# Sorted attention and a mixture of experts in one program: earlier q heads, a shorter set-up path, and expert weights that wait for rows

## The chip, the cores and the metric

The kernel runs as one program on one core of one Trainium2 chip. The number that counts is the device time of that program in microseconds (us). The kernel before took 233.02 us as the median of three runs (231.26 to 235.55).

The engines are named as in the profile: PE is TensorE, with PEld for its weight loads; DVE is VectorE, ACT is ScalarE, POOL is GpSimd, SP is SyncE. A "q" behind a name (SPq, POOLq) is that engine's own instruction queue.

## The reference, cut to what matters

The program is two stages, one after the other. First comes an attention in blocks: a small matrix per head is normalised in rows and columns five times (Sinkhorn), blocks of k and v are mixed by it, and each of 8 blocks of 96 tokens attends to its own mixed block. Then a mixture of 8 experts works on the attention's output: each token goes to the one expert that its gate prefers.

```python
# q, k, v: (4, 8, 768, 64), sort_net: (4, 8, 8, 8); 8 blocks of 96 tokens
P = sort_net
for _ in range(5):
    P = P - max_row(P); P = exp(P)
    P = P / (row_sum(P) + 1e-09)
    P = P / (column_sum(P) + 1e-09)
k_sorted = einsum('bhij,bhjcd->bhicd', P, k_blocks)
v_sorted = einsum('bhij,bhjcd->bhicd', P, v_blocks)
attn = softmax(q_blocks @ k_sorted^T / sqrt(64))
x = (attn @ v_sorted) as (3072 tokens, 512)

# w_gate: (512, 8), modality_bias: (2, 8), w1: (8, 512, 1024), w2: (8, 1024, 512)
logits = x @ w_gate + modality_bias[modality_id]
e_idx  = argmax(logits)
gate_w = softmax(logits)[e_idx]
for e in range(8):
    h = relu(x[e_idx == e] @ w1[e])
    out[e_idx == e] = gate_w * (h @ w2[e])
```

## The kernel before

The attention is cut into 32 **units**: unit u works on two batches (g = u // 16), one half of the blocks, and one head (u % 8). Per unit, TensorE makes scores, ScalarE their exponential (L407), TensorE the product with v (`av`), and VectorE divides by the row sums, which writes 64 columns of the x tile `xb` (L424). Eight units fill one x tile of 8 x 96 tokens. The tile goes through the gate: four transposed pieces (`gate_T`) and four small products (`gate_L`), then `choose` and `place`, and its rows are scattered to a scratch array in HBM, sorted by expert, by eight indirect transfers of GpSimd. A `table` says which groups of 256 rows are full. Such a group is read back, transposed, as `xT`, and run through an expert. Experts are renumbered by the modality bias so that the two that will get nearly all tokens stand first; `home_pick` and `home_map` work this out. Slots 0, 2, 4, ... use the first one's weights, slots 1, 3, 5, ... the second one's.

The expert work is a list of **pieces**: `mL1` (8 matmuls of the first layer) and `mL2` (8 of the second). From unit 18 on, pieces are mixed in between the attention's steps.

```python
def load_q(g, hh):                      # four heads of two batches
    t = q_in(g, hh).rearrange("p (r h f) -> p r h f", r=2, h=4)
    return [nc.gpsimd.dma_start(out=t[:, par], in_=q[2 * g + par, 4 * hh:4 * hh + 4]
                                .rearrange("h (p t) d -> p h (t d)", t=6)) for par in range(2)][0]

def spread_q(g, hq, eng=None):          # reorders two heads in SBUF, L125
    ...
    for z in range(2):
        (eng or nc.vector).tensor_copy(il[:, z], t[:, :, (hq % 2) * 2 + z].rearrange("p r t d -> p t r d"))

load_q(0, 0)
...
load_k(0, 0); load_k(0, 1); load_v(0)
load_q(0, 1)
...
spread_q(0, 0, nc.gpsimd)
spread_q(0, 1, nc.gpsimd)
# ... cut ...
for u in range(4):
    tq_pe(u)                            # TensorE turns a head of q, L231
for it in range(5):                     # Sinkhorn on VectorE, exponential on ScalarE (L245)
    ...
    if it == 3: tq_out(0, nc.scalar.copy)
    if it == 4:
        for u in range(1, 4): tq_out(u, nc.scalar.copy)
    ...
make_bd(0)                              # block matrix of P for the sort, last line L276
# ... cut ...
def mod_rows():
    src = modI.rearrange("b (r t w) -> b t r w", r=16, t=6)[:, :, :, 0]
    nc.vector.tensor_copy(modB, src)                                    # L297
    tp = mipsum.tile([128, 64], BF16, tag="mi", name="modT")
    nc.tensor.transpose(tp[0:BLK, 0:NTL], modB..., ident[0:NTL, 0:NTL])  # L299
    nc.vector.tensor_copy(modF, tp[0:BLK, 0:NTL])

def gate_consts():
    red_w = perm_mult(wgf, wg_sb, "w")           # the gate's weights in the new order
    nc.gpsimd.tensor_scalar(modN, modF, -1.0, 1.0, ALU.mult, ALU.add)
    # ... three GpSimd operations make biasm, the bias of every token ...
    def rest_w():
        red_w()
        nc.vector.tensor_copy(wgp, wgf)
    return rest_w

def prep_s(u):
    if 4 <= u < 32 and not (u // 8) % 2 and u % 2 == 0:
        spread_q(u // 16, (u % 8) // 2)
        use(dve=0.7)
# ... cut ...
scores(0); expo(0)
home_pick(); home_map()
mod_rows()
load_k(1, 0); load_k(1, 1)
wait_w = gate_consts()
make_bd(1)
scores(1); expo(1)
late_consts()
...
for n, (f, g, x0, kd) in enumerate(g0[8:]):   # the sort of v, L358, copied out at L336
    f(g, x0, kd)
load_v(1); load_q(1, 0); load_q(1, 1)
zero_block()
av(0)
wait_w()
prep_s(4)
# ... cut: what is done at which unit ...
at2(9, place, 0)
for t in range(1, 8):
    at1(9 + t, lambda t: ones_[0](t), t)                 # scatter t of the first x tile
    if t == 3: at1(9 + t, lambda: load_w(0, parts=(0,)))
at1(16, table_x, 0)
at1(16, lambda: load_w(0, parts=(1,)))
at1(16, lambda: load_w(1))
at1(18, place, 1)
# ... cut ...
for u in range(2, 32):
    p1, p2 = pace(u)                    # (0, 0) below unit 18, then (1, u % 2)
    scores(u); expo(u)
    for f, a in A1.get(u, []): f(*a)
    run_pieces(p1)
    av(u - 1)
    prep_q(u + 2)
    prep_s(u + 3)
    for f, a in A2.get(u, []): f(*a)
    run_pieces(p2)
run_pieces(1); av(31)
run_pieces(2); gate_T(3, 3)
run_pieces(1); gate_L(3, 3); choose(3)
run_pieces(2); place(3)
for t in range(1, 8):
    run_pieces(2)
    ones_[3](t)
table_x(3)
run_pieces(1000)                        # all that is left
```

Of the kernel before, what the change touches and what calls it, by code (L numbers as in the profile page):

```python
# [17 lines left out]
def kernel(  # L18
# [13 lines left out]
    nc = tc.nc  # L32
# [80 lines left out]
    def load_v(g):  # L113
        nc.gpsimd.dma_start(out=v_in, in_=v_src[g * 128:(g + 1) * 128])

    def load_q(g, hh):
        t = q_in(g, hh).rearrange("p (r h f) -> p r h f", r=2, h=4)
        return [nc.gpsimd.dma_start(out=t[:, par], in_=q[2 * g + par, 4 * hh:4 * hh + 4]
                                    .rearrange("h (p t) d -> p h (t d)", t=6)) for par in range(2)][0]

    def spread_q(g, hq, eng=None):
        t = q_in(g, hq // 2).rearrange("p (r h t d) -> p r h t d", r=2, h=4, t=6)
        il = q_il[hq % 2].rearrange("p (h t r d) -> p h t r d", h=2, t=6, r=2)
        for z in range(2):
            (eng or nc.vector).tensor_copy(il[:, z], t[:, :, (hq % 2) * 2 + z].rearrange("p r t d -> p t r d"))  # L125
# [1 line left out]
    sI = singles.tile([128, 32], I32)  # L127
    pI = singles.tile([128, 1], I32)
    idI = singles.tile([BLK, NTL], I32)
    load_q(0, 0)  # L130
    nc.gpsimd.iota(sI, pattern=[[1, 32]], base=0, channel_multiplier=0)
    make_identity(nc, ident)
    load_k(0, 0)
    load_k(0, 1)
    load_v(0)
    load_q(0, 1)
    jI = singles.tile([1, 4], I32)
    hI = singles.tile([1, 4], I32)
    nc.gpsimd.iota(pI, pattern=[[0, 1]], base=0, channel_multiplier=1)
# [1 line left out]
    nc.gpsimd.iota(jI, pattern=[[1, 2], [0, 2]], base=0, channel_multiplier=0)  # L141
    nc.gpsimd.iota(hI, pattern=[[PR, 2], [CAP, 2]], base=0, channel_multiplier=0)
    spread_q(0, 0, nc.gpsimd)
    spread_q(0, 1, nc.gpsimd)

    ones_bf = singles.tile([128, 128], BF16)
    ones8 = singles.tile([128, E], FP32)
# [86 lines left out]
    def tq_out(u, eng):  # L234
        g, h = u // 16, u % 8
        qT = qTb[g][:, h * 768:(h + 1) * 768].rearrange("p (i t r) -> p i t r", i=NB, t=6)
        eng(qT, tq.pop(u).rearrange("p t (i r) -> p i t r", r=16))

    for u in range(4):
        tq_pe(u)  # L240
    for it in range(5):
        if it == 0:
            nc.vector.tensor_reduce(red, P_t, AX.X, ALU.max)
            nc.vector.tensor_tensor(P_t, P_t, red.broadcast_to([BH, NB, NB]), ALU.subtract)
        nc.scalar.activation(P_t, P_t, ACT.Exp)  # L245
        if it == 3:
            tq_out(0, nc.scalar.copy)
        if it == 4:
            for u in range(1, 4):
                tq_out(u, nc.scalar.copy)  # L250
        for f in gap[it]:
            f()
        nc.vector.tensor_reduce(red, P_t, AX.X, ALU.add)
        nc.vector.reciprocal(red, red)
        nc.vector.tensor_tensor(P_t, P_t, red.broadcast_to([BH, NB, NB]), ALU.mult)
        nc.vector.tensor_reduce(red, P_swap, AX.X, ALU.add)
        nc.vector.reciprocal(red, red)
# [41 lines left out]
        nc.tensor.transpose(tp[0:BLK, 0:NTL], modB.rearrange("b t r -> b (t r)"), ident[0:NTL, 0:NTL])  # L299
# [4 lines left out]
    def gate_consts():  # L304
        red_w = perm_mult(wgf, wg_sb, "w")
        nc.gpsimd.tensor_scalar(modN, modF, -1.0, 1.0, ALU.mult, ALU.add)
# [9 lines left out]
        def rest_w():  # L316
            red_w()
            nc.vector.tensor_copy(wgp, wgf)
        return rest_w

    busy = [0.0, 0.0]

# [54 lines left out]
        return u // 16, (u // 8) % 2, u % 8  # L377

    def prep_s(u):
        if 4 <= u < 32 and not (u // 8) % 2 and u % 2 == 0:  # L380
            spread_q(u // 16, (u % 8) // 2)
            use(dve=0.7)

    def prep_q(u):
        if 4 <= u < 32 and not (u // 8) % 2:
            tq_pe(u)
            tq_out(u, nc.scalar.copy if pick(0.8, 0.56) else nc.vector.tensor_copy)

# [220 lines left out]
    def w_views(z):  # L609
        o = z * WCOL  # L610
        return (w01[:, o:o + 4 * F].rearrange("p (c f) -> p c f", c=4),
                w01[:, o + 4 * F:o + WCOL].rearrange("p (c f) -> p c f", c=8))

    def load_w(z, tab=None, n=None, parts=(0, 1)):
        tb, n = (etab, z) if tab is None else (tab, n)
        er = nc.values_load(tb[0:1, n:n + 1], engines=(PoolEng,), min_val=0, max_val=E - 1)
        v1, v2 = w_views(z)
        if 0 in parts:
            nc.gpsimd.dma_start(out=v1, in_=moe_w1[bass.ds(er, 1)].rearrange("o (c p) f -> p (o c) f", p=128))
        if 1 in parts:  # L620
            nc.gpsimd.dma_start(out=v2, in_=moe_w2[bass.ds(er, 1)].rearrange("o (c p) f -> p (o c) f", p=128))

    def stage_of(s):
        return 0 if s < 2 else 1 if s < 4 else 2 if s < 8 else 3
# [1 line left out]
    xins = {}  # L626
# [99 lines left out]
    def late_consts():  # L726
        pt = singles.tile([128, 2], I32)
        nc.vector.tensor_scalar(pt[:, 0:1], pI, 15, None, ALU.bitwise_and)
        nc.vector.tensor_scalar(pt[:, 1:2], pI, 4, None, ALU.logical_shift_right)
        ptf = singles.tile([128, 1], FP32)  # L730
        ptc = singles.tile([128, 2], FP32)
        nc.vector.tensor_copy(ptc, pt)
        nc.vector.scalar_tensor_tensor(ptf, ptc[:, 0:1], 6.0, ptc[:, 1:2], ALU.mult, ALU.add)
        nc.vector.tensor_scalar(idI, idI, ptf[0:BLK], None, ALU.add)
        nc.vector.tensor_scalar(sF256, sF[0:1], float(PR), None, ALU.mult)
        nc.vector.tensor_copy(JC.rearrange("p a b -> p (a b)"), jI)
        nc.vector.tensor_copy(HC.rearrange("p a b -> p (a b)"), hI)
        use(dve=1.6)
# [9 lines left out]
    expo(0)  # L748
    home_pick()
    home_map()  # L750
    mod_rows()
    load_k(1, 0)
    load_k(1, 1)
    wait_w = gate_consts()
    make_bd(1)
    scores(1)
    expo(1)
    late_consts()
    use(dve=-busy[1], act=-busy[0])
    for n, (f, g, x0, kd) in enumerate(g0[8:]):  # L760
        f(g, x0, kd)
    load_v(1)
    load_q(1, 0)
    load_q(1, 1)
    zero_block()
    av(0)
    wait_w()
    prep_s(4)

    st = {"tab": -1, "x": 0, "l1": 0, "done": 0, "pos": 0}  # L770

# [21 lines left out]
    def at1(u, f, *a):  # L793
        A1.setdefault(u, []).append((f, a))

    def at2(u, f, *a):
        A2.setdefault(u, []).append((f, a))

    at2(8, lambda: nc.vector.memset(v_sb[1][:, :, D:D + 1], 1.0))
    for m in range(4):  # L800
        for c in range(4):
# [15 lines left out]
    for t in range(1, 8):  # L817
        at2(17 + t, lambda t: ones_[1](t), t)
# [42 lines left out]
    for u in range(2, 32):  # L861
        p1, p2 = pace(u)
        scores(u)
        expo(u)
        for f, a in A1.get(u, []):
            f(*a)
        run_pieces(p1)
        av(u - 1)
        prep_q(u + 2)
        prep_s(u + 3)  # L870
        for f, a in A2.get(u, []):
            f(*a)
        run_pieces(p2)
    run_pieces(1)
    av(31)
    run_pieces(2)
    gate_T(3, 3)
    run_pieces(1)
    gate_L(3, 3)
    choose(3)  # L880
    run_pieces(2)
    place(3)
    for t in range(1, 8):
        run_pieces(2)
        ones_[3](t)
    table_x(3)
    run_pieces(1000)
# [75 lines left out]
```

## Time and profile before

| Engine | busy, us | share of the span of 231.7 us |
|---|---|---|
| PE (matmul) | 164.9 | 71% |
| PEld (weight load) | 122.8 | 53% |
| DVE | 104.7 | 45% |
| ACT | 94.3 | 41% |
| POOL | 76.1 | 33% |

The profiled execution took 231.7 us from its first to its last instruction, with a mean granted TensorE clock of 0.846. The transfers moved 27.67 MB.

The profile page cuts the span into 40 equal slices, and gives for each slice the busy tenths of every engine, the TensorE clock that was granted in tenths of full speed (PEclk), and the GB/s moved. The chain that ended last is followed back from the last instruction, at each step to what released it; its lines give start, length and what. A line of the timeline gives start, length, engine, source line, operation, what is written from what, the number of instructions, and in brackets the idle time before it with what ended it. A line of the waits gives who waited for whom, the sum in us, how often, and the longest.

### The profile page before, as it was taken

The page shows a single profiled execution, that of the slowest core. Times are in us where ns is not written, and L with a number is a line of the kernel's source. Part 1 is how long each engine was busy: PE and PEld are TensorE (multiplying, and loading weights), DVE is VectorE, ACT ScalarE, POOL GpSimd, SP SyncE. Part 2 cuts the span into 40 slices and gives each one's busy share as a digit, 9 for nine tenths or more (in the row PEclk, how much of TensorE's full clock was granted, in tenths as well). Part 3 has the DMA queues.
Part 4 walks back from the last instruction along what each step waited for, and adds up shares of the span by engine and source line. Part 5 has one row for each costly group of instructions (what it writes and reads, how often), then busy time and mean ns, then how long its engine had stood idle before and what let it go on. Part 6 is the DMA issues. An engine that isn't in the chain of part 4 may idle for free.

```text
span 231.7 us, 5104 instructions
## 1 busy us (share of the span) xinstructions
PE 164.9 (71%) x2023; PEld 122.8 (53%) x2023; DVE 104.7 (45%) x340; ACT 94.3 (41%) x147; POOL 76.1 (33%) x102
## 2 busy tenths in 40 slices
PE   0265667995999600298889888999990999999600
PEld 0154565985889500286565657668660576674200
DVE  5868866657548660044566436233270133232100
ACT  2264445665577710075464626443341132322300
POOL 7621515000434420031633465337651031333300
PEclk9997587569569955569999999999998699999965
DMA  5999999990119399981215323594364642212200
GB/s 69 208 228 203 218 213 174 198 184 3 36 36 162 101 150 184 191 138 37 108 48 129 97 75 121 127 145 148 96 214 97 105 103 96 92 45 91 89 15 0
DMA packets 30129, 27.67 MB, mean 119 GB/s; under 512 B 18799, under 2 KB 25743, under 8 KB 29840
## 3 DMA queue, kind: packets, MB, share of 16 engines
q0 software_dynamic: 11760, 23.10, 45.7%
q1 hardware_dynamic: 18336, 4.16, 11.8%
q8 instruction: 18, 0.29, 0.6%
q14 instruction: 15, 0.12, 0.2%
HBM read 27.35 MB, written 10.52 MB: 163 GB/s over the span
## 4 chain that ended last, share of the span: by engine, by line
PE 54%; DVE 16%; DMA 13%; issue 5%; POOL 3%; ACT 2%; SPq 1%; POOLq 0%; DVEq 0%
PE hp L663 19%; PE yp L686 15%; DMA xT<-xs_scratch 10%; PE ka L349 3%; PE gt L433 3%; DVE xb L424 3%; PE va L358 3%; PE op L420 3%; PE sc L401 2%; PE lg L439 2%; DMA xs_scratch<-zpad 2%; PE tq L231 1%; POOL xs_scratch L510 1%; DMA xs_scratch<-xb,dest 1%; DVE v_sb L336 1%
## 5 line engine op out<-in xcount | busy, mean ns | idle before, releaser
L663 PE MATMUL hp<-xT,w 128*128 128x256 bf16 x384 | 50.1, 284 | 18.5 <-DMA xT<-xs_scratch 18.4
L510 POOL DMA_INDIRECT xs_scratch<-xb,dest x32 | 29.6, 925 | 68.5 <-issue 33.6
L663 PEld LDWEIGHTS <-w 128*128 128x128 bf16 x384 | 37.6, 102 | 27.1 <-issue 12.6
L677 POOL DMA_INDIRECT out_dram<-kvb,idg x25 | 24.6, 985 | 54.5 <-ACT kvb L673 27.3
L407 ACT ACTIVATE attnT<-sc 96x768 bf16<-96x768 f32 x32 | 25.8, 806 | 10.8 <-PE sc L401 10.6
L657 ACT ACTIVATE hT<-hp 128x512 bf16<-128x512 f32 x17 | 10.1, 596 | 35.7 <-PE hp L663 35.6
L686 PE MATMUL yp<-w,qT 128*128 128x512 bf16 x96 | 22.9, 383 | 0.0
L424 DVE TENSOR_TENSOR xb<-op,rs 96x512 bf16<-96x512 f32 x32 | 22.0, 687 | 1.7 <-DMA xs_scratch<-xb,dest 0.6
L686 PE MATMUL yp<-w,hT 128*128 128x512 bf16 x96 | 22.5, 379 | 0.0
L423 DVE RECIPROCAL rs<-op 96x8 f32<-96x8 f32 x32 | 6.4, 199 | 30.5 <-PE op L420 29.1
L673 ACT ACTIVATE kvb<-yp,idg 128x512 f32<-128x512 f32 x15 | 10.3, 687 | 21.5 <-PE yp L686 21.5
L231 PE MATMUL tq<-ident,q_il 128*128 128x128 bf16 x96 | 10.8, 270 | 10.7 <-POOL q_il L125 10.3
L420 PE MATMUL op<-v_sb,attnT 96*128 96x65 bf16 x256 | 15.1, 207 | 2.1 <-DVE v_sb L336 1.3
L358 PE MATMUL va<-bd,kvb 128*128 128x128 bf16 x128 | 14.6, 285 | 1.4 <-ACT v_sb L336 0.8
L675 DVE TENSOR_SCALAR kvb<-yp,idg 128x512 f32<-128x512 f32 x9 | 6.8, 751 | 19.5 <-PE yp L686 19.5
L401 PE MATMUL sc<-qT,kT 64*128 64x96 bf16 (+1 forms) x256 | 12.9, 228 | 3.0 <-issue 1.1
L420 PEld LDWEIGHTS <-attnT 96*128 96x128 bf16 x256 | 12.8, 107 | 4.2 <-DVE v_sb L336 1.4
L657 ACT ACTIVATE qT<-hp 128x512 bf16<-128x512 f32 x15 | 9.0, 597 | 14.1 <-PE hp L663 14.0
L336 ACT CAST v_sb<-va 96x512 bf16<-96x512 f32 (+1 forms) x20 | 11.9, 629 | 6.7 <-PE va L358 6.5
L433 PE MATMUL gt<-ident,xb 96*128 96x96 bf16 x128 | 9.8, 230 | 6.6 <-DVE xb L424 5.7
L686 PEld LDWEIGHTS <-qT 128*128 128x128 bf16 x96 | 9.3, 100 | 9.5 <-issue 0.5
L358 PEld LDWEIGHTS <-kvb 128*128 128x128 bf16 x128 | 13.2, 189 | 2.0 <-issue 1.8
(176 smaller groups left out, 213.2 us busy)
## 6 DMA issues: line engine op xcount, KB each, us to landing
w<-in_moe_w_dram POOLq DMA_DIRECT2D x4, 1024.0 KB, 15.8
kvb<-in_k_dram POOLq DMA_DIRECT2D x4, 768.0 KB, 12.1
kvb<-in_v_dram POOLq DMA_DIRECT2D x2, 1536.0 KB, 10.7
v_sb<-in_q_dram POOLq DMA_DIRECT2D x4, 384.0 KB, 14.6
q_in<-in_q_dram POOLq DMA_DIRECT2D x4, 384.0 KB, 13.2
xs_scratch<-zpad SPq DMA_DIRECT2D x3, 258.0 KB, 3.4
xs_scratch<-xb,dest POOLq DMA_INDIRECT x32, 2.6
out_dram<-kvb,idg POOLq DMA_INDIRECT x25, 2.9
```

The costliest lines, as they stand in the source:

```text
L336: (nc.scalar.copy if pick(act, dve) else nc.vector.tensor_copy)(dst, src)
L358: nc.tensor.matmul(acc[:, z], v_cols[:, d0 + z], bd[g], start=True, stop=True)
L401: nc.tensor.matmul(sc[0:m, par, j * BLK:(j + 1) * BLK], kT[g][rows, x0:x0 + m], qT[rows, i], start=True, stop=True)
L407: mark[0] = nc.scalar.activation(attnT[u % 2][:, 0:8 * BLK].rearrange("p (r f) -> p r f", r=2), sc_tiles.pop(u)[0:BLK, :, 0:4 * BLK], ACT. ...
L420: nc.tensor.matmul(ov[:, par, j], attnT[u % 2][:, c0:c0 + 128], v_sb[g][0:BLK, par * 64 + h * 8 + i, 0:D + 1], start=True, stop=True)
L424: nc.vector.tensor_tensor(xt[:, :, h * D:(h + 1) * D].rearrange("p (r j) d -> p r j d", r=2), ov[0:BLK, :, :, 0:D], rs.broadcast_to([BLK, ...
L433: nc.tensor.transpose(tp[:, t], xb[m % 2][:, t, c * 128:(c + 1) * 128], ident[:BLK, :BLK])
L510: ins = nc.gpsimd.indirect_dma_start(out=xs_dram, out_offset=bass.IndirectOffsetOnAxis(ap=dest[:, t:t + 1], axis=0), in_=xt.bitcast(I32)[: ...
L657: mark[0] = nc.scalar.activation(dst, src, ACT.Relu)
L663: nc.tensor.matmul(hp[:, f], w_at(s, c * F + (2 * j + f) * 128, 128), xT_b[s % NX][:, c], start=(c == 0), stop=(c == 3))
L677: ins = nc.gpsimd.indirect_dma_start(out=out, out_offset=bass.IndirectOffsetOnAxis(ap=idg[:, t, 0:1], axis=0), in_=y, in_offset=None, boun ...
L686: nc.tensor.matmul(yp, hT_b[s % 2][:, fc, t * 128:(t + 1) * 128], w_at(s, 4 * F + fc * Dm, Dm), start=(fc == 0), stop=(fc == 7))
```

## The change

There are five parts. (1) The first transfer of q brings two heads instead of four, and only these two are spread and turned before the sort; heads 2 and 3 follow behind v. The later spreads of the first half's q, which VectorE did, go to GpSimd. (2) The modality rows, the bias of every token, the second block matrix and the late constants move from before unit 1 to after the first `av` and into units 2 to 4, so that TensorE and VectorE meet fewer set-up steps on the way to the sort of v. (3) The first expert's weights are loaded between the second half's q, well before the first rows are scattered. (4) The second expert's weights are issued in unit 17 and wait there until the rows of slot 1 have been read back. (5) In each unit the expert pieces come ahead of the gate's steps, so there is work between the norm of an x tile and the gate's transposes of it; the scatters of the first tile come one step later, and fewer pieces are done between the last scatters.

The `load_w` function also returns its transfers, so that part 4 can name them.

```diff
-    load_q(0, 0)
+    load_q(0, 0, 2)
     nc.gpsimd.iota(sI, ...)
     make_identity(nc, ident)
     load_k(0, 0)
     load_k(0, 1)
     load_v(0)
-    load_q(0, 1)
+    load_q(0, 2, 2)
+    load_q(0, 4, 4)
 ...
     spread_q(0, 0, nc.gpsimd)
-    spread_q(0, 1, nc.gpsimd)
 ...
-    for u in range(4):
+    for u in range(2):
         tq_pe(u)
 ...
         if it == 4:
-            for u in range(1, 4):
-                tq_out(u, nc.scalar.copy)
+            tq_out(1, nc.scalar.copy)
 ...
     def prep_s(u):
-        if 4 <= u < 32 and not (u // 8) % 2 and u % 2 == 0:
+        if 16 <= u < 32 and not (u // 8) % 2 and u % 2 == 0:
 ...
     def prep_q(u):
-        if 4 <= u < 32 and not (u // 8) % 2:
+        if 2 <= u < 32 and not (u // 8) % 2:
 ...
     home_map()
-    mod_rows()
     load_k(1, 0)
     load_k(1, 1)
-    wait_w = gate_consts()
-    make_bd(1)
+    wait_w = gate_w()
     scores(1)
     expo(1)
-    late_consts()
     use(dve=-busy[1], act=-busy[0])
     for n, (f, g, x0, kd) in enumerate(g0[8:]):
         f(g, x0, kd)
+    spread_q(0, 1, nc.gpsimd)
     load_v(1)
-    load_q(1, 0)
-    load_q(1, 1)
+    load_q(1, 0, 4)
+    load_w(0, parts=(0,))
+    load_q(1, 4, 4)
+    load_w(0, parts=(1,))
+    spread_q(0, 2, nc.gpsimd)
     zero_block()
+    prep_q(2)
     av(0)
+    prep_q(3)
     wait_w()
-    prep_s(4)
+    mod_rows()
 ...
+    def late_w1():
+        for i, ins in enumerate(load_w(1)):
+            if i == 0:
+                tc.add_manual_dep(ins.ins, xins[1].ins.name, SYNC, reason="rows of the first slots go ahead")
 ...
-    at2(9, place, 0)
+    at2(2, lambda: (gate_bias(), spread_q(0, 3, nc.gpsimd)))
+    at2(3, make_bd, 1)
+    at2(4, late_consts)
+    at1(10, place, 0)
     for t in range(1, 8):
-        at1(9 + t, lambda t: ones_[0](t), t)
-        if t == 3:
-            at1(9 + t, lambda: load_w(0, parts=(0,)))
-    at1(16, table_x, 0)
-    at1(16, lambda: load_w(0, parts=(1,)))
-    at1(16, lambda: load_w(1))
+        at2(9 + t, lambda t: ones_[0](t), t)
+    at2(16, table_x, 0)
+    at2(17, late_w1)
     at1(18, place, 1)
 ...
         scores(u)
         expo(u)
+        run_pieces(p1)
         for f, a in A1.get(u, []):
             f(*a)
-        run_pieces(p1)
         av(u - 1)
         prep_q(u + 2)
         prep_s(u + 3)
+        run_pieces(p2)
         for f, a in A2.get(u, []):
             f(*a)
-        run_pieces(p2)
     run_pieces(1)
     av(31)
-    run_pieces(2)
+    run_pieces(1)
     gate_T(3, 3)
     run_pieces(1)
     gate_L(3, 3)
     choose(3)
-    run_pieces(2)
+    run_pieces(1)
     place(3)
     for t in range(1, 8):
-        run_pieces(2)
+        run_pieces(1)
         ones_[3](t)
     table_x(3)
     run_pieces(1000)
```

`gate_w` and `gate_bias` are the two halves of the old `gate_consts`.

More of the change, by code (lines that the diff above doesn't have):

```diff
@@ L114, in load_v, with load_q @@
         nc.gpsimd.dma_start(out=v_in, in_=v_src[g * 128:(g + 1) * 128])
[L116 to L119, printed above, removed]
+    def load_q(g, h0, nh):
+        t = q_in(g, h0 // 4).rearrange("p (r h f) -> p r h f", r=2, h=4)
+        z = h0 % 4
+        for par in range(2):
+            nc.gpsimd.dma_start(out=t[:, par, z:z + nh], in_=q[2 * g + par, h0:h0 + nh]
+                                .rearrange("h (p t) d -> p h (t d)", t=6))
     def spread_q(g, hq, eng=None):
@@ L302, with gate_w, rest_w, gate_bias @@
     wgf = small.tile([128, 4, E], FP32, tag="wgf", name="wgf")
-    def gate_consts():
+    def gate_w():
         red_w = perm_mult(wgf, wg_sb, "w")
+        def rest_w():
+            red_w()
+            nc.vector.tensor_copy(wgp, wgf)
+        return rest_w
+    def gate_bias():
         nc.gpsimd.tensor_scalar(modN, modF, -1.0, 1.0, ALU.mult, ALU.add)
@@ L314, in gate_consts @@
         nc.gpsimd.tensor_tensor(biasm, biasm, tmp, ALU.add)
[L316 to L319, printed above, removed]
     busy = [0.0, 0.0]
@@ L617, in load_w @@
         v1, v2 = w_views(z)
+        res = []
         if 0 in parts:
-            nc.gpsimd.dma_start(out=v1, in_=moe_w1[bass.ds(er, 1)].rearrange("o (c p) f -> p (o c) f", p=128))
+            res.append(nc.gpsimd.dma_start(out=v1, in_=moe_w1[bass.ds(er, 1)].rearrange("o (c p) f -> p (o c) f", p=128)))
         if 1 in parts:
-            nc.gpsimd.dma_start(out=v2, in_=moe_w2[bass.ds(er, 1)].rearrange("o (c p) f -> p (o c) f", p=128))
+            res.append(nc.gpsimd.dma_start(out=v2, in_=moe_w2[bass.ds(er, 1)].rearrange("o (c p) f -> p (o c) f", p=128)))
+        return res
     def stage_of(s):
```

## The prediction

> **What bounds the kernel now.** I read the page's parts 1 and 2 first, then the chain that ended last, the waits, and the timeline around every wait that the chain passes through. Busy shares say little: TensorE is busy 71% of 231.7 us. The slices of part 2 say where it isn't (5.8 us each):
>
> ```profile
> PE   0265667995999600298889888999990999999600
> ...
> PEclk9997587569569955569999999999998699999965
> ...
> GB/s 69 208 228 203 218 213 174 198 184 3 36 36 162 101 150 184 191 138 37 108 48 129 97 75 121 127 145 148 96 214 97 105 103 96 92 45 91 89 15 0
> ```
>
> TensorE is empty at the start (set-up), in slices 15 to 17 of 40 (from about 81 to 97 us), in slice 31 (174 to 180), and at the end. In slices 15 to 17 the transfers run at 150, 184 and 191 GB/s, in slices 10 to 12 at 3, 36 and 36. The chain of waits tells what is waited for in the hole:
>
> ```profile
> 77.86 2.68 DMA xs_scratch<-xb,dest
> ...
> 80.75 15.98 DMA xT<-xs_scratch
> ...
> 96.86 1.87 PE hp L663 x8
> ```
>
> The first 256 routed rows are read back transposed (xT), and that took 15.98 us. The timeline shows what lay in front of it, and one such read later, with nothing in front:
>
> ```profile
> 78.91 0.94 POOL L621 DMA_DIRECT2D w<-in_moe_w_dram  x1
> ...
> 80.10 0.79 POOL L619 DMA_DIRECT2D w<-in_moe_w_dram  x1 [0.25 <-issue]
> ...
> 80.89 1.01 POOL L621 DMA_DIRECT2D w<-in_moe_w_dram  x1
> ...
> 84.06 10.53 SPq L630 DMA_TRANSPOSE xT<-xs_scratch  x1
> ...
> 122.54 1.28 SPq L630 DMA_TRANSPOSE xT<-xs_scratch  x1
> ```
>
> Three weight transfers of 1024 KB were issued within 3 us just ahead of the rows. The read-back at 122.54 landed in 3.25 us by the chain. So the hole is contention, not dependence. The second hole is in the chain's last part, and small waits come from the waits of TensorE between 97 and 170 us:
>
> ```profile
> 171.24 3.82 DMA xs_scratch<-zpad
> 175.19 4.67 DMA xT<-xs_scratch
> 179.91 3.59 PE hp L663 x16
> ```
> ```profile
> PE hp L663 <- DMA xT<-xs_scratch: 12.6, 1, 12.6
> PE gt L433 <- DVE xb L424: 4.7, 5, 1.1
> PE gt L433 <- DVE tb_ti L556: 0.7, 1, 0.7
> ```
>
> The last says that the gate's transposes waited 5.4 us in six pieces for the normalised x tile. From 180 to 218 us TensorE is busy 37.42 of 38 us; nothing there can be gained. The last 14 us are the output's drain and the program's end, which the change leaves. One early wait is on the list too:
>
> ```profile
> 24.98 0.26 PE L299 MATMUL modT<-ident,modB 32*96 32x32 bf16 x1 [2.18 <-DVE modB L297]
> ...
> 25.22 0.50 PE L401 MATMUL sc<-qT,kT 64*128 64x96 bf16 x8
> ...
> 37.43 0.82 PE L231 MATMUL tq<-ident,q_il 128*128 128x128 bf16 x6 [0.38 <-DVE q_il L125]
> ```
>
> **What the skill says.** The Trainium skill, "DMA: Bandwidth & Descriptors", section "Queues, rings and completion order": each DMA engine takes turns between the queues that have work, a packet at a time. The trace agrees: the rows go on SyncE's queue, the weights on GpSimd's, and many small packets of rows each waited a turn of weights (15.98 against 3.25 us). So holding the weights back should free the rows. The Trainium skill, "TensorE: Matmul & The Clock Gate", section "What's actually happening": the clock is half until about 3.4 us of sustained work, and falls back after an idle window. The trace agrees in kind: after the first hole eight L663 matmuls took 1.87 us, later 0.87 to 0.99, and after the second sixteen took 3.59 against 1.75. But it also shows half clock from 58 to 68 us (granted 0.50) with TensorE busy 9.79 of 10 us, so I can't say when it recovers. "SBUF — State Buffer", section "Who interferes with whom": VectorE and GpSimd share a port pair that one holds alone. The trace fits: while GpSimd copied q (9.41 to 12.54 us) the line L255 took 0.75 us once, against 0.21 elsewhere, and L260 0.39 against 0.21.
>
> **The change part by part.**
>
> *Start, 0 to 35 us.* Half of the first q goes ahead and GpSimd copies two heads, not four, before the Sinkhorn ends. q isn't what the first sort waits for (that is bd, written at 15.23 us). Only the two lengthened VectorE instructions matter: 0.54 + 0.18 us, of which about half, 0.3 us. Next, modT leaves the path. Then the scores of unit 1 wait only for the exponential of unit 0 to free their PSUM tile (it ends at 23.65) and start at 23.7 instead of 25.22: 1.5 us. The sort of v behind them takes 9.5 us by itself: four double tiles in one buffer, each about 0.95 us of matmuls and 1.03 to 1.23 us of copy. It just starts earlier. Gain 1.8 us at av(0), at 33.4 instead of 35.18.
>
> *35 to 45 us: given back.* The spreading of heads 4 to 7 moves from VectorE (two copies, 0.93 us) to GpSimd (0.82 us a copy), and stands there behind the issue of everything. From the end of the v sort at 32.1 (33.86 less 1.8), 0.3 to start: v 0.60, two q 1.50, w1 about 1.1 (0.80 and 0.3 of gap), two q 1.50, w2 1.2 gives 38.3, and the first copy ends at 39.1. The transposes of head 4 started at 37.43 before; scores(3), next in TensorE's order, moves from 38.18 to about 39.8. mod_rows also makes TensorE wait some 1.2 us for VectorE after av(0), but that is swallowed by the longer wait. So the gain of 1.8 turns into a loss of about 1.6 us. Spreading heads 6 and 7, after 2.3 us of bias work (0.21 + 0.62 + 0.67 + 0.76), ends near 43.9, about when they are needed at 44; no more loss. The first expert's weights now go into the idle slices 10 to 12 or just ahead of them; v lands before them.
>
> *The first hole.* place(0) after the scores of unit 10 hides about 0.4 us, so unit 16 starts at 77.4 instead of 76.2. Its last scatter goes out 1.7 us later and lands in 2.2 us (the quickest in the trace took 2.1; no weights are ahead), 0.3 us to the read, 3.3 us to land: 84.9. Before, the first expert matmul started at 96.86. Gain 12.0 us. TensorE reaches that point at about 82, so 3 us of waiting stay, about what place(1) waited for choose(1) before.
>
> *Second expert's weights.* They are issued when rows 256 to 511 have landed, 2.6 us later (spacing of the two reads at 122.54 and 125.20): 87.5. The quickest weight landing in the trace is 9.4 us, so w1 is there at 97.5, w2 5 us after. The first use is in unit 22: 98.73 to 112.29 before from the same point, 13.6 less 0.7 of gate wait, from about 86.8: 99.7. Slack 2 us for w1, more for w2 (unit 25). No new wait, but thin.
>
> *Gate waits.* A first-layer piece (0.87 us) now stands between the norm and the gate's transposes, at least as long as most of the six waits (0.7 to 1.1). 5.4 us less about 1.0 for the tighter hand-overs of tables 1 and 2, whose rows land only 5 to 6 us after their tables: 4.4 us.
>
> *The end.* The tail runs 11 pieces before the last table instead of 20, so 14 of the 46 pieces that need no last rows are left instead of 5: ten of 0.88 and four of 1.73, 15.7 us. The rows of the last table took from 167.87 (its matmul) to 179.9, that is 12.0 us. Covered. Gain: the wait of 5.8 us, and the half clock behind it, 1.6 us, less 0.6 because only one piece covers choose(3). 6.8 us.
>
> Sum: 12.0 + 4.4 + 6.8 = 23.2 us; the start's changes are inside the first term. 233.0 − 23.2 = 209.8, and I say 210.
>
> **Rivals.** (1) *GpSimd's queue becomes the wait.* It now runs q copies at 39 us in program order, and stands still in unit 17 until rows have landed, with the next scatters behind it. For it: my 39.1 is built of issue times and any of them may be longer; if the spread ends at 42 the start loses 3 us more. Against it: scatters of the second part left at 86.20 before, and only have to be there by unit 24. Time 212 to 215. (2) *Late weights.* If w1 needs the 15.8 us that is the median of its landings, unit 22 waits 4 to 5 us and w2 as much again: 214 to 218. Against it: that median has three transfers queued at once, here two. (3) *The clock.* It ran half from 36 to 51 and from 58 to 68 us. If the new waits near 39 us keep it half longer, or place(0)'s shorter wait keeps it full after 58, that is 3 us either way: 207 to 213. (4) *Rows were slow for another reason* than weights, say their own small packets: then the hole stays and only the other parts remain, 222. The read at 122.54 speaks against it.
>
> **Range and chances.** Each large term rests on a wait the trace shows whole and a replacement measured elsewhere in it, so I see little chance of no gain. The errors add on the slow side: 205 to 218. Faster by over 2% (under 228.4): 0.95; within 2%: 0.03; slower: 0.02.
>
> **What would show it.** xT lands 3 to 4 us after issue near 85 us and the empty slices there go, apart from 2 to 3 us. No modT wait before the v sort; a wait of tq for q_il on GpSimd near 37 to 39 us. The waits gt for xb nearly vanish after 97 us. No wait of hp for xT near the end, and the same stretch of about 52 us from the last expert part's first matmul to the end, some 1.6 us less for the clock. Wrong would be: hp waiting for w, GpSimd's copies ending past 41 us, or rows that still take over 6 us.

## The result, and the profile after

The changed kernel takes 213.83 us (median of four, 213.73 to 214.21) against 232.97 us (231.26 to 235.55) for the kernel before: a ratio of 0.9204, with a 95% interval of 0.9154 to 0.9255. The time lies in the predicted range, 3.8 us above the predicted 210.0. The profiled span went from 231.7 to 212.5 us, and the granted clock from 0.846 to 0.879.

First the page's slices after the change. Each of the 40 is now 5.3 us long: busy tenths of TensorE, its granted clock in tenths, and GB/s.

```profile
PE   0119674799779981999986998899999999999200
...
PEclk9999887556955997599996999999999999999955
...
GB/s 60 211 227 206 209 218 227 202 202 208 207 97 51 32 38 68 50 177 174 260 84 155 37 107 107 122 151 173 205 162 146 166 74 85 85 63 102 60 2 0
```

The hole of three empty slices has shrunk to one (slice 16, 80 to 85 us), and the wait near the end has gone. Two digits are new. Slices 21 and 22 (106 to 117 us) show 8 and 6, where the kernel before had 8s and 9s from slice 18 to the wait near the end. The clock, too, dips to 6 in slice 22.

Next the chain that ended last, with start, length and what the time went to:

```profile
78.51 3.45 DMA xs_scratch<-xb,dest
...
84.80 3.33 DMA xT<-xs_scratch
...
91.05 12.81 DMA xs_scratch<-xb,dest
...
106.54 2.37 DMA xs_scratch<-xb,dest
109.11 4.04 DMA xT<-xs_scratch
113.19 1.66 PE hp L668 x8
```

The read at 84.80 is the one of slot 1, whose landing the second expert's weights wait for. The read-back of the first rows goes out ahead of it on SyncE's queue:

```profile
82.03 1.35 SPq L635 DMA_TRANSPOSE xT<-xs_scratch  x1
```

The matmul that waits for these rows starts at 85.42, so the read, 15.98 us before, now takes 3.39 at most. The chain does not jump over the whole middle any more, though. It goes through the scatters of the second x tile and the reading of their rows (109.11), and then through a wait of TensorE that the kernel before did not have. The first of those scatters stands behind the second expert's two weight transfers in GpSimd's queue, and took 12.81 us to land.

The waits of TensorE between 97 and 170 us (who waited for whom, sum in us, how often, longest):

```profile
PE hp L668 <- DMA xT<-xs_scratch: 2.4, 1, 2.4
PE rk L484 <- DVE oh L468: 0.7, 1, 0.7
PE op L423 <- DVE xb L427: 0.6, 1, 0.6
```

The six waits of the gate (`gt` for `xb` and `tb_ti`, 5.4 us) have all left the list. One of 2.4 us for rows and two short ones have come.

Last the timeline of TensorE at the places that the prediction named, with the idle time before each group in brackets:

```profile
38.49 0.82 PE L233 MATMUL tq<-ident,q_il 128*128 128x128 bf16 x6 [1.93 <-POOL q_il L127]
...
85.42 1.87 PE L668 MATMUL hp<-xT,w 128*128 128x256 bf16 x8 [4.34 <-DMA xT<-xs_scratch]
...
113.19 1.66 PE L668 MATMUL hp<-xT,w 128*128 128x256 bf16 x8 [2.42 <-DMA xT<-xs_scratch]
```

The span divides into three stretches at two events that both kernels have: the first expert matmul, and the matmul of the last table (`cp`, L538 before and L541 after; it starts at 167.9 before and at 146.2 after). Nine pieces moved from ahead of that table to behind it: seven of 0.875 us and two of 1.735, that is 9.6 us. The two later stretches are compared with these put back.

| stretch | before | after | after, like for like | difference | predicted |
|---|---|---|---|---|---|
| start to first expert matmul | 96.86 | 85.42 | 85.42 | −11.4 | −12.0 |
| to the last table | 71.0 | 60.8 | 70.4 | −0.6 | −3.8 |
| to the end | 63.8 | 66.3 | 56.7 | −7.1 | −7.4 |
| sum | 231.7 | 212.5 | 212.5 | −19.2 | −23.2 |

In the predicted column, the 0.6 us that the prediction took off the end for `choose(3)` stands in the second stretch, where it falls by this division. Two stretches came out within 0.6 us. Of the 4.0 us that are missing, 3.2 are in the middle one.

### The profile page after: what moved, and what is told of

It reads as the page before. It is cut to its first block, busy times and chain, and to the rows that moved or that the text cites. A ratio compares the mean times of both kernels' runs of the same rounds, so it can differ in the third digit from the quotient of the medians.

```text
span 212.5 us, 5100 instructions
## 1 busy us (share of the span) xinstructions
PE 162.4 (76%) x2012; PEld 123.2 (58%) x2023; DVE 103.3 (49%) x337; ACT 93.7 (44%) x146; POOL 80.1 (38%) x108
## 4 chain that ended last, share of the span: by engine, by line
PE 45%; issue 17%; DMA 12%; DVE 8%; POOL 7%; ACT 2%; SPq 1%; POOLq 1%; DVEq 0%
PE yp L691 16%; PE hp L668 16%; DMA xs_scratch<-xb,dest 9%; DMA xT<-xs_scratch 3%; POOL xs_scratch L513 3%; PE ka L352 3%; PE va L361 2%; PE sc L404 2%; PE gt L436 2%; PE op L423 1%; DVE P_t L256 1%; PE tq L233 1%; ACT v_sb L339 1%; POOL w L625 1%; PE ypl L721 1%
## 5 line engine op out<-in xcount | busy, mean ns | idle before, releaser
L668 PE MATMUL hp<-xT,w 128*128 128x256 bf16 x384 | 49.0, 280 | 6.8 <-DMA xT<-xs_scratch 6.8
L668 PEld LDWEIGHTS <-w 128*128 128x128 bf16 x384 | 37.0, 100 | 15.1 <-issue 6.9
L691 PE MATMUL yp<-w,hT 128*128 128x512 bf16 x90 | 21.9, 379 | 0.4 <-issue 0.2
L680 DVE TENSOR_SCALAR kvb<-yp,idg 128x512 f32<-128x512 f32 x12 | 9.0, 750 | 24.1 <-PE yp L691 22.3
L233 PE MATMUL tq<-ident,q_il 128*128 128x128 bf16 x96 | 10.2, 259 | 11.5 <-POOL q_il L127 11.5
L662 ACT ACTIVATE hT<-hp 128x512 bf16<-128x512 f32 x18 | 10.8, 597 | 16.1 <-PE hp L668 16.0
L662 ACT ACTIVATE qT<-hp 128x512 bf16<-128x512 f32 x17 | 10.2, 597 | 15.6 <-PE hp L668 14.9
L678 ACT ACTIVATE kvb<-yp,idg 128x512 f32<-128x512 f32 x12 | 8.2, 687 | 17.4 <-PE yp L691 17.4
L691 PEld LDWEIGHTS <-hT 128*128 128x128 bf16 x96 | 9.1, 98 | 9.0
L233 PEld LDWEIGHTS <-q_il 128*128 128x128 bf16 x96 | 7.4, 117 | 11.9 <-POOL q_il L127 11.9
```

Of the source, the lines that this page charges most:

```text
L233: nc.tensor.transpose(tp[:, t], src[:, t], ident)
L662: mark[0] = nc.scalar.activation(dst, src, ACT.Relu)
L668: nc.tensor.matmul(hp[:, f], w_at(s, c * F + (2 * j + f) * 128, 128), xT_b[s % NX][:, c], start=(c == 0), stop=(c == 3))
L691: nc.tensor.matmul(yp, hT_b[s % 2][:, fc, t * 128:(t + 1) * 128], w_at(s, 4 * F + fc * Dm, Dm), start=(fc == 0), stop=(fc == 7))
```

## The experiments

The theory after the result had four parts. (T1) The hole at 81 us was weights in front of rows, and the order of the transfers alone removes it. (T2) The pieces ahead of the gate's steps do remove the gate's waits, but these waits had hidden the arrival of the second tile's rows; TensorE now comes to slot 2 before them. (T3) The fourteen pieces kept for the tail cover the last rows. (T4) The new start is worth next to nothing, since its gain is given back at 38 us. The rivals: the rows of slot 2 are late because the second expert's weights stand in the scatters' queue and block GpSimd (against T2); the start is worth 2 us or more (against T4); the part-5 order is worth nothing (against T2's first half).

Each experiment changes the kernel after, where nothing else is said. They ran on three chips, and the kernel before was timed on each: 244.76 us (243.91 to 249.37) on the first, 231.94 (230.30 to 234.71) on the second, 245.31 (240.76 to 247.51) on the third. On the first and third chips the profiles show ScalarE and VectorE waiting one to seven times, up to 5.8 us at a time, for an event whose source is not in the trace; on the second there is only one such wait, of 1.8 or 1.9 us, in the drain of the output, as in the kernel after above. So the first and third chips are called disturbed below; differences of a few microseconds are taken from the second chip alone, and from the other two only what a trace shows of one wait.

### The weights without their wait

```diff
     def late_w1():
         for i, ins in enumerate(load_w(1)):
-            if i == 0:
-                tc.add_manual_dep(ins.ins, xins[1].ins.name, SYNC, reason="rows of the first slots go ahead")
+            pass
```

> The changed kernel (213.8 us), but the second expert's weights are issued in unit 17 at once and do not wait for the rows. Theory (weights in flight delay the rows): the first xT read takes over 9 us instead of 3.3, the first expert matmul starts near 92 instead of 85.4, and the time is about 220. Rival (the rows are slow by their own small packets, the wait brings nothing): 213.8, xT again in 3 to 4 us.

Measured on the first chip: 239.48 us (236.24 to 242.09), ratio to the kernel before 0.9713 (0.9577 to 0.9849). In the chain of this kernel the first read of rows and the matmuls behind it are:

```profile
83.66 12.44 DMA xT<-xs_scratch
96.23 1.86 PE hp L668 x8
```

The hole is back: 12.44 us for the read of the first rows, which took 3.39 at most with the wait in place, and 13.30 us of idle TensorE ahead of the matmul at 96.23, against 4.34. The expectation had that matmul near 92. Chip and disturbance are not the cause: two kernels below that keep the wait have their first expert matmul at 84.77 and 84.34 on this chip, and take 226.95 and 227.83 us. Here two transfers of 1 MB stand in front, not three as in the kernel before; two are enough. T1 holds for the wait.

### The kernel before with the order of weights alone

This is the kernel before with parts 3 and 4 of the change and nothing else (`load_w` and `late_w1` as in the change's diff).

```diff
     load_q(1, 0)
+    load_w(0, parts=(0,))
     load_q(1, 1)
+    load_w(0, parts=(1,))
 ...
-        if t == 3:
-            at1(9 + t, lambda: load_w(0, parts=(0,)))
     at1(16, table_x, 0)
-    at1(16, lambda: load_w(0, parts=(1,)))
-    at1(16, lambda: load_w(1))
+    at2(17, late_w1)
```

> The kernel before with nothing changed but the weights: the first expert's load between the second half's q, the second expert's issued in unit 17 after the rows of slot 1. Theory (the first hole is contention with weights and goes by itself): the first expert matmul near 84.5 instead of 96.9, the wait at the last table stays at about 5 us, time 220 to 221.5. Rival (it takes the other parts to make use of it): over 225.

Measured on the third chip: 232.26 us (231.51 to 233.43), ratio 0.9577 (0.9477 to 0.9676). The first read-back is sent at 82.45 and the first expert matmul starts at 85.81, so it takes 3.36 us at most. That nothing waits for xT there says less, since on this disturbed chip TensorE comes late to the place (the scores of unit 18 at 83.29 against 80.56 in the kernel before). The gate's waits stay, and so does the wait near the end. From this kernel's list of TensorE's waits from 97 us on:

```profile
PE gt L433 <- DVE xb L424: 7.6, 4, 2.9
PE hp L665 <- DMA xT<-xs_scratch: 5.6, 1, 5.6
PE gt L433 <- DVE tb_ti L556: 0.7, 1, 0.7
```

So parts 3 and 4 alone close the first hole, which is the second half of T1. The ratio, taken over to the 233 us of the kernel before on a quiet chip, would be a gain of some 10 us (232.97 × 0.0423 = 9.9) and a time of 223.1, near the 11.4 of the first stretch but between the 220 to 221.5 of the theory and the 225 of the rival. That conversion between chips is an estimate.

### The changed kernel again, on the second chip

> The changed kernel itself, unaltered, as the measure for the others of this group. On the chip of the first group the kernel before took 244.8 us instead of 233.0, with waits of some us on queues outside the program, so times of that group can't be set against 213.8. All theories: 0.92 of the kernel before on the same chip; on a chip like the first one 213.8.

Measured: 213.93 us (213.31 to 215.05), ratio 0.9241 (0.9180 to 0.9301). The two waits for rows are there again: 4.60 us at 84.90 and 2.20 us at 112.21, with the first eight matmuls at half clock behind each (1.86 and 1.87 us). The last scatter of the second tile goes out at 105.92. This run is the measure for the next three.

### The second expert's weights long before

Here they are loaded in unit 4, without a wait, so that no weight stands between the two tiles' scatters.

```diff
     at2(4, late_consts)
+    at2(4, lambda: load_w(1))
 ...
-    at2(17, late_w1)
```

> The changed kernel, but the second expert's weights are issued in unit 4, right behind the first expert's, and wait for nothing. Theory (in the changed kernel the 2 MB stand in front of the second part's scatters on GpSimd's queue, 12.8 us to landing for the first, and make the read of slot 2 late): scatters land in 2 to 3 us, the wait of hp for xT at slot 2 falls from 2.4 to about 1.3 us, the time is 1 to 1.5 us below the changed kernel. Rival 1 (TensorE simply comes too early there): the same time. Rival 2 (the 2 MB now delay the first part's scatters and with them slot 0): 1 us or more slower, the first expert matmul after 86 us.

Measured: 214.53 us (213.34 to 215.24), ratio 0.9256 (0.9195 to 0.9317): no gain. The chain of this kernel, at the second tile's rows:

```profile
106.83 2.39 DMA xs_scratch<-xb,dest
109.41 4.56 DMA xT<-xs_scratch
```

and what the last scatter waited for:

```profile
106.83 0.92 POOL L513 DMA_INDIRECT xs_scratch<-xb,dest  x1 [0.66 <-ACT qT L662]
```

The scatters now begin at 89.08 us instead of 90.55 and nothing stands in front of them, yet the last one goes out at 106.83, no sooner than the 105.92 of the kernel after on this chip, and TensorE waits 2.79 us for the rows. The last scatter is held up here by ScalarE's work of its unit, which ends at 106.57, and not by the queue; in the kernel after's first trace that work ends at 106.12 and the scatter goes out at 106.54. The 12.81 us in the chain of the kernel after therefore made the rows late by a few tenths at most. The rival to T2 falls. So does the worry that the wait holds GpSimd up for too long: without its 9.36 us of standing still nothing is gained.

### One piece fewer in unit 25

If TensorE reaches slot 2 before its rows, then a unit of attention put between should fill the wait. One piece is left out of unit 25 and done later.

```diff
     def pace(u):
-        return (0, 0) if u < 18 else (1, u % 2)
+        return (0, 0) if u < 18 else (1, u % 2 if u != 25 else 0)
```

> The changed kernel, with one expert piece less in unit 25 (all later pieces come one step later, one more is left for the end). Theory (TensorE comes 2.4 us too early to slot 2, and the idle time costs half clock behind it): the wait goes, the eight L668 matmuls of slot 2 take about 0.9 us instead of 1.66, the time is 2.5 to 3.5 us below the changed kernel. Rival (the wait only moves, to slot 4 or to the last table): within 0.7 us of the changed kernel.

Measured: 210.38 us (209.08 to 210.75), ratio 0.9072 (0.9013 to 0.9131). All four of its runs lie below all four of the kernel after on the same chip; the medians differ by 3.55 us. TensorE's timeline for this kernel, with the scores of the unit ahead:

```profile
111.66 0.34 PE L404 MATMUL sc<-qT,kT 64*128 64x96 bf16 x8
112.41 1.03 PE L668 MATMUL hp<-xT,w 128*128 128x256 bf16 x8 [0.41 <-DMA xT<-xs_scratch]
```

and the same place of the kernel after on this chip:

```profile
109.66 0.34 PE L404 MATMUL sc<-qT,kT 64*128 64x96 bf16 x8
112.21 1.87 PE L668 MATMUL hp<-xT,w 128*128 128x256 bf16 x8 [2.20 <-DMA xT<-xs_scratch]
```

Slot 2 starts at the same moment in both, because the rows come when they come. But in the new one another unit's scores and product have been done by then, the wait is 0.41 us instead of 2.20, and the clock stays full. From 112.3 to 142 us the granted clock is 1.00 instead of 0.95, on 28 us of busy TensorE some 1.4 us. The waits do not fall by the whole 1.8 us: a new one of 0.88 us, of the gate's product `lg` for ScalarE, has come, and some short ones have gone. From 97 to 142 us TensorE is idle for 2.22 us instead of 4.17. The 1.95 us and the 1.4 of clock make 3.3, and TensorE's last matmuls start 3.19 us earlier in this pair of traces (191.96 against 195.15). T2 is shown, and this kernel is faster than the kernel before and the kernel after.

### The start of before with the rest of the change

The first q, the spreads, the modality rows, the bias and the late constants stand as in the kernel before; parts 3, 4 and 5 stay.

```diff
-    load_q(0, 0, 2)
+    load_q(0, 0)
 ...
-    load_q(0, 2, 2)
-    load_q(0, 4, 4)
+    load_q(0, 1)
     spread_q(0, 0, nc.gpsimd)
+    spread_q(0, 1, nc.gpsimd)
 ...
     home_map()
+    mod_rows()
 ...
-    wait_w = gate_w()
+    wait_w = gate_consts()
+    make_bd(1)
```

> The changed kernel with the old start: four heads of q first and spread by GpSimd ahead of the Sinkhorn's end, heads 4 to 7 spread by VectorE, modality rows, bias, second block matrix and late constants before unit 1. The weights' order, the order of the pieces and the tail are the changed kernel's. Theory (the new start gains 2 us to the first av and gives all of it and a little more back behind GpSimd's queue): av(0) near 35.2 instead of 33.1, scores of unit 16 near 76.2 instead of 76.8, time 0 to 1 us below the changed kernel. Rival (the shorter set-up path is what is worth something): 1.5 to 2.5 us above it.

Measured: 213.31 us (211.53 to 213.44), ratio 0.9191 (0.9128 to 0.9254). The first expert matmul starts at 85.52, with a wait of 4.65 us for xT, against 84.90 and 4.60. The new start has its first `av` at 33.03 instead of 36.38 (35.2 had been expected), but `scores(3)` at 39.14 instead of 39.45, and the scores of unit 16 at 76.07 instead of 76.63: of 3.35 us gained, 0.3 are left at 39 us. So the new start brings nothing measurable, and parts 1 and 2 could be left out. T4 holds; that the gain becomes a loss, as the theory had it, is not shown.

### Two pieces between the last scatters again

```diff
     av(31)
-    run_pieces(1)
+    run_pieces(2)
 ...
     choose(3)
-    run_pieces(1)
+    run_pieces(2)
     place(3)
     for t in range(1, 8):
-        run_pieces(1)
+        run_pieces(2)
         ones_[3](t)
```

> The changed kernel, with two expert pieces instead of one at the places of the tail (20 pieces before the last table, not 11). Theory (the pieces left over cover the way of the last rows): a wait of hp for xT of 5 to 6 us returns near the end, followed by half clock, time 220 to 221. Rival (the last rows come earlier for another reason, such as an emptier transfer queue): under 216.

Measured on the first chip: 226.95 us, ratio 0.9264 (0.9156 to 0.9371). The kernel after wasn't timed on this chip, so the price of the edit stays open. Its timeline near the end shows the mechanism:

```profile
173.18 3.50 PE L668 MATMUL hp<-xT,w 128*128 128x256 bf16 x16 [3.63 <-DMA xT<-xs_scratch]
```

TensorE waits again for the last rows, and sixteen matmuls take 3.50 us where 1.91 are usual. Wait and half clock are 5.2 us together. T3 holds, with a smaller wait than the 5.8 us of before and the 5 to 6 expected.

### The pieces behind the gate's steps again

```diff
         expo(u)
-        run_pieces(p1)
         for f, a in A1.get(u, []):
             f(*a)
+        run_pieces(p1)
         av(u - 1)
         prep_q(u + 2)
         prep_s(u + 3)
-        run_pieces(p2)
         for f, a in A2.get(u, []):
             f(*a)
+        run_pieces(p2)
```

It ran twice, on the first and on the third chip.

> The changed kernel, with the expert pieces behind the gate's steps again, as before the change; all else kept. Theory (the order hides the gate's waits, about 5.4 us, but brings TensorE sooner to rows that are not there, so that about half of it is paid back): the waits of gt for xb return with 4 to 5 us, the wait of hp for xT at the third slot (2.4 us) goes, time 216 to 217. Rival 1 (the full 5.4 us is gained): 219. Rival 2 (the order is worth nothing): 213.8.

> The pieces behind the gate's steps again, as in b_order, whose times were disturbed. The changed kernel is at 213.9 on a quiet chip. Theory (the order hides 5.4 us of gate waits and pays about half back at slot 2): 216 to 217, with 4 to 6 us of waits of gt for xb and of rk for the choice, and under 1 us of hp for xT at slot 2. Rival 1 (all of it gained): 219. Rival 2 (worth nothing): 213.9.

Measured: 236.40 us on the first chip, too scattered for an interval (229.84 to 238.26), and 233.50 (231.46 to 234.17) on the third, ratio 0.9609 (0.9495 to 0.9724). In microseconds the worth of the order stays open. TensorE's waits from 97 us on, second run:

```profile
PE gt L436 <- DVE xb L427: 3.8, 3, 1.7
PE gt L436 <- DVE rs L426: 2.1, 1, 2.1
...
PE gt L436 <- DVE tb_ti L559: 0.7, 1, 0.7
PE hp L668 <- DMA xT<-xs_scratch: 0.2, 1, 0.2
```

Without the new order the gate's waits are back (6.6 us in five pieces on this disturbed chip), and the wait for slot 2's rows is 0.2 us instead of 2.2 to 2.4. The three other traces with the old order (the first run, the kernel before, the weights' order alone) show no wait for these rows at all; all eight with the new order and the pace of the kernel after show one of 2.2 to 2.9 us, on all chips. This is the exchange that T2 claims: the order takes the gate's waits away, and part of them turns up as one wait for rows.

### The late spreads of q on VectorE

```diff
-    spread_q(0, 2, nc.gpsimd)
 ...
     wait_w()
+    spread_q(0, 2)
+    use(dve=0.7)
     mod_rows()
 ...
-    at2(2, lambda: (gate_bias(), spread_q(0, 3, nc.gpsimd)))
+    at2(2, lambda: gate_bias())
+    at2(3, lambda: (spread_q(0, 3), use(dve=0.7)))
```

> The changed kernel, with heads 4 to 7 of q spread on VectorE again instead of GpSimd. Theory (the spread stands behind GpSimd's transfer issues and holds TensorE 1.9 us at the turning of head 4): that wait shrinks below 0.6 us, the scores of unit 3 start near 38.0 instead of 39.2, time 212.4 to 212.9. Rival (something else there, such as the modality rows or the clock, sets the pace): 213.6 to 214.

> Heads 4 to 7 of q spread on VectorE, as in d_dve, whose times were disturbed; there the scores of unit 3 began at 37.92 instead of 39.24. Theory (that start is carried through to the end, since the chain of scatters follows TensorE): 212.4 to 213.0 against 213.9. Rival (it is lost again before unit 16, by waits or clock): 213.5 to 214.2.

Measured: 227.83 us on the first chip, ratio 0.9320 (0.9228 to 0.9411), and 232.81 (226.82 to 233.23, no interval) on the third. In the traces the wait of `tq` for GpSimd has gone in both, and `scores(3)` starts at 37.92 and 37.78 instead of 39.24. In its place the wait of `modT` for VectorE has grown from 1.42 to 2.17 us, in both. The first expert matmul is at 84.34 on the first chip, 0.6 to 1.1 us earlier than in the two traces of the kernel after, and at 87.21 on the third. Whether this helps is not settled.

### Faster scatters of the first tile, with the pace of unit 25

```diff
     for t in range(1, 8):
-        at2(9 + t, lambda t: ones_[0](t), t)
-    at2(16, table_x, 0)
+        at2(10 + t // 2, lambda t: ones_[0](t), t)
+    at2(14, table_x, 0)
```

The pace of unit 25 is edited as above.

> The changed kernel with one piece less in unit 25 (210.4 by itself) and the first x tile's scatters two to a unit instead of one, its table in unit 14 instead of 16. Theory (what is left of the first hole, 4.6 us of hp waiting for xT and 1 to 2 us of half clock behind it, is set by the pace of the scatters): the first rows are there when unit 18 begins, the wait goes, time 204 to 206. Rival (the rows' own way or VectorE's table work sets it, or the closer scatters delay units 10 to 14): over 208.5.

Measured on the third chip: 224.23 us (223.11 to 226.60), ratio 0.9226 (0.9091 to 0.9361), the fastest of the kernels on that chip. At the first slot its timeline shows:

```profile
85.86 1.05 PE L668 MATMUL hp<-xT,w 128*128 128x256 bf16 x8
```

There is no wait for rows there, and the clock is full again, after standing at half from 71.4 to 85.0 us. But this does not settle the theory, because TensorE comes to the place 5.6 us later than the 80.3 us of the kernel after on the second chip. On its way ScalarE waits for an event from outside the trace:

```profile
74.31 1.06 ACT L339 CAST v_sb<-va 96x512 bf16<-96x512 f32 x2 [4.23 <-remote]
```

What does come earlier is the read-back, sent at 78.38 us against 81.57; the last scatter went out at 72.33 against 77.74. So the pace of the scatters and the table sets a part of the hole at 81 us; how much of it would go without the disturbance is open. Whether this beats the 210.38 us of the paced kernel on a quiet chip was not measured.

## Why the prediction was right, and where it was off

**The first hole: right.** Predicted a first expert matmul at 84.9, measured 85.42. Its pieces moved against each other: unit 16 came at 76.84 instead of 77.4, the last scatter landed in 3.45 us instead of 2.2, the read in 3.39 at most (3.3 predicted). The 2.2 us had been the quickest landings of the trace, said to hold since no weights are ahead. In the kernel with the weights loaded in unit 4 and in the paced one it took 4.00 and 3.74 us, so the size was wrong and the weights have no part in it. TensorE waits 4.34 us there instead of the 3 predicted. The runs show that the read is slow while weights are in flight, 15.98 us behind three loads and 12.44 behind two; that each packet of rows waits a turn of weights, as the prediction reads it, no trace here shows.

**Start, and the part given back: right.** Predicted `av(0)` at 33.4, and it came at 33.14. The copy on GpSimd that `tq` waits for was predicted to end at 39.1, `tq` started at 38.49; `scores(3)` came at 39.24, predicted 39.8. The gain is given back, as the step says. That it becomes a loss of 1.6 us is not shown. `scores(3)` is 1.1 us later than in the trace of the kernel before (38.18), but with the old start in the changed kernel it comes 0.3 us later still, and the time is the same within the spread of the runs.

**Second expert's weights: right.** Issued at 88.78 (predicted 87.5), first used at 99.61 (99.7), and no matmul waited for them.

**Gate waits: the step that was mis-sized.** It said that 5.4 us of waits would go, less "about 1.0 for the tighter hand-overs of tables 1 and 2": 4.4, and 0.6 for `choose(3)`. The first number was right, since all six waits went. The second was far too low. The hand-over of table 1 costs 2.42 us of wait and, behind it, 3.4 us at half clock (the first eight matmuls take 1.66 us against 1.05), and two other short waits came to 1.3. In the middle stretch TensorE's idle time fell only from 5.70 to 4.28 us, and its busy time, with the nine pieces put back, rose from 65.3 to 66.1: that is the 0.6 us measured like for like. What I had not done was to compare, for slot 2, TensorE's own work with the way of the rows once the gate's waits were out of it. From the table's matmul to the first one of slot 2 the kernel before took 6.7 us without a wait for rows, gate waits included. After the change TensorE has 5.2 us of its own work in there and the rows take 7.6. The prediction noted that the rows land only 5 to 6 us after their tables, and drew too little from it. Two runs show this: with the old order the wait for rows falls to 0.2 us and the gate's waits return, and with one piece taken out of the way there is 3.55 us to be had.

**The end: right.** Predicted 15.7 us of pieces to cover the last rows, and they last from 146.25 to 162.06, 15.8 us; nothing waits. From the last rows' first matmul to the end it is 50.4 us against 51.8, where 1.6 us less was predicted for the clock.

**The rivals.** GpSimd's queue, late weights and slow rows for another reason all failed to come. GpSimd's halt of 9.36 us stands in the trace, but loading early instead gains nothing, and its copy at 39 us ended before the 41 us that would have been a sign. The clock rival was half right: the half clock from 58 us on is still there in the page (slices 12 and 13 have 5), and the new wait at slot 2 brought a new stretch of 3.4 us.

## What to carry to other kernels

A wait that is removed from a busy engine moves everything behind it earlier, so the next hand-over whose slack is smaller than that wait becomes the new wait: set, for each hand-over behind it, the engine's own work against the transfer's way before the gain is counted. A large load that isn't needed yet should not be in flight when small rows are read: here it could wait for them, because its first use was far enough away, or go long ahead of them (213.93 and 214.53 us). If a wait remains where work from another stream is at hand, moving a single piece past it can be worth more than the wait, because the clock stays up as well.

## What the runs showed of the hardware

- In each of the eight traces in which TensorE waited 2.2 to 2.9 us for the rows of slot 2, the granted clock went to 0.50 once and stayed there for 3.4 us. It fell between 0.2 us before the end of the wait and 1.5 us after it. So the half clock is in the first eight matmuls (1.66 and 1.87 us in the kernel after, instead of 1.03 to 1.05) or comes later. In the kernel without the weights' wait, for one, the first eight are fast and the next eight slow:

```profile
125.57 1.03 PE L668 MATMUL hp<-xT,w 128*128 128x256 bf16 x8 [2.31 <-DMA xT<-xs_scratch]
...
127.68 1.89 PE L668 MATMUL hp<-xT,w 128*128 128x256 bf16 x8
```

- Behind the wait of 0.41 us (one piece fewer in unit 25) the clock stayed full. At 1.8 to 2.1 us it went either way: half clock followed a wait of 1.78 us (weights' order alone, at 105.11) and did not follow one of 2.14 (spreads on VectorE, third chip, at 162.46). The Trainium skill, "TensorE: Matmul & The Clock Gate", section "What's actually happening", puts the fall to half clock after an idle window of about 3.4 us. The runs agree in kind, and the stretch at half clock has that length, but idle times of 2.2 to 2.9 us were enough for it.
- A read-back of 256 rows took 3.2 to 3.4 us for the first slot in the kernel after and its variants on the second chip, and 3.4 to 4.6 us for slot 2 (4.56 where the second expert's weights had been loaded long before); it took 3.25 us for slot 2 in the kernel before.
- While GpSimd copied q during the Sinkhorn steps, one small VectorE instruction (L256) took 1.30 us instead of 0.21, more than the 0.75 of the kernel before.
- A scatter of 96 rows behind two loads of 1 MB in the same queue landed 12.81 us after its start; the others of which a landing is shown in this kernel took 2.4 to 3.5.
- The kernel before took about 13 us more on two of the three chips (244.76 and 245.31 against 231.94 us), in company with the waits for events from outside the trace; that these make all of the difference is not shown.
